# Centred-only transposes at the start, and attention pieces in front of score bursts, in a transformer layer on one core

## Chip, cores, metric

The kernel runs on one core of one Trainium2 chip. The metric is the device time of one execution in microseconds; medians of several executions are quoted. Spans in the profile are 1.5 to 2.0 us shorter than the timed execution. The record marks a run as slow when it is over 1.5% above the fastest of its kernel.

## The reference

One pre-norm layer in bf16 with 2048 tokens and width 1024: attention with 32 heads of 32 and a causal window of 256, then an MLP of width 3584 with SiLU, both with a residual.

```python
def _layernorm(x, axis=-1, eps=1e-5):
    m = jnp.mean(x, axis=axis, keepdims=True)
    v = jnp.var(x, axis=axis, keepdims=True)
    return (x - m) / jnp.sqrt(v + eps)
...
x = A_x
h = x + _A_ref(_layernorm(x, axis=-1), A_wqkv, A_wo)     # q, k, v; windowed softmax; wo
h2 = h + _B_ref(_layernorm(h, axis=-1), B_w1, B_w2)      # silu(h @ w1) @ w2
```

## The kernel before

Tokens go in four blocks of 512, each of four row tiles of 128. TensorE (PE) computes V (a `v_group` per row tile and half of the columns), then Q and K (`qk_group`), of block b+1 as dense 128x512 matmuls, and the attention of block b is sprinkled between them: *bursts* of scores (tiles of 32 rows) and *pieces* of attention output (33 columns each). Block 0 has nothing to hide behind: its row tiles must be normalized and transposed first. Tiles 0 to 2 are transposed on PE, tile 3 by DMA.

```python
    load_x(0, 0)
    load_wqkv(2 * D)                 # first half of the V columns, 1 MB
    load_x(0, 1, nc.scalar)          # issued from ScalarE's queue
    load_x(0, 2)
    load_wqkv(2 * D + 512)
    load_x(0, 3)
    load_wqkv(0)
...  # 11 warm-up matmuls
    ln_stats(x_ring[0], st, 0)
    ln_root(st, rs, 0)
...
    v_group(0, 1, 0, act, turn_1_rest)
    ln_first(x_ring[2], st, rs, 2, 1)
    ln_stats(x_ring[3], st, 3)
    ln_root(st, rs, 3)
    ln_first(x_ring[3], st, rs, 3, 1)
    ln_transpose(x_ring[3], lnT_b[0], 3)      # by DMA
    for c0 in (D, 512, D + 512):
        load_wqkv(c0)
...
    for j in range(4):
        load_x(1, j)                          # block 1
...
    class Stream:
        def between(self, kt):                # called before each dense matmul
            if self.seen * self.n >= self.done * 192:
                self.bursts[self.done]()
                self.done += 1
            if self.seen * self.n * 2 >= (self.given * 2 + 1) * 192:   # halfway between bursts
                if pending:
                    pending.pop(0)()                                   # a piece
...
```

While Q and K of block 0 run, VectorE takes the statistics of block 1 in the same queue as the evacuations (copies of finished results out of PSUM) of the odd Q/K groups. Two PSUM banks serve these groups in turn.

The softmax here doesn't subtract the row's maximum and nothing guards it: scores larger than these inputs give would overflow.

Of the kernel before, what the change touches and what calls it, by code (L numbers as in the profile page):

```python
# [9 lines left out]
F32 = mybir.dt.float32  # L10
I32 = mybir.dt.int32
ACT = mybir.ActivationFunctionType
ALU = mybir.AluOpType

P = 128
# [29 lines left out]
def kernel(  # L45
# [49 lines left out]
    def view(region, off, *dims):  # L95
        n = 1
        for d in dims:
            n *= d
        ap = region[:, off:off + n]
        if len(dims) == 2:  # L100
            return ap.rearrange("p (a b) -> p a b", b=dims[1])
        if len(dims) == 3:
            return ap.rearrange("p (a b c) -> p a b c", b=dims[1], c=dims[2])
        return ap
# [29 lines left out]
    def load_x(b, j, queue=nc.sync):  # L134
        queue.dma_start(out=x_ring[(b % 2) * 4 + j], in_=x2d[(b * 4 + j) * P:(b * 4 + j + 1) * P, :])  # L135

    def load_wqkv(c0):
        dst = wqk[:, :, c0:c0 + 512] if c0 < 2 * D else wv[:, :, c0 - 2 * D:c0 - 2 * D + 512]
        nc.sync.dma_start(out=dst, in_=wqkv_v[:, :, c0:c0 + 512])

    eps = const.tile([P, 1], F32, name="eps")
    nc.vector.memset(eps[:], LN_EPS)
# [1 line left out]
    nc.scalar.activation(out=dummy[:], in_=eps[:], func=ACT.Sqrt)  # L144

    load_x(0, 0)
    load_wqkv(2 * D)
    load_x(0, 1, nc.scalar)
    load_x(0, 2)
    load_wqkv(2 * D + 512)  # L150
    load_x(0, 3)
    load_wqkv(0)

    ident = const.tile([P, P], BF16, name="ident")
    make_identity(nc, ident[:])
    warm = view(r_e, 0, 2, 512)
    nc.vector.memset(warm, 0.0)
    nc.gpsimd.memset(v[:, :, :, DH:VW], 1.0)


    for i in range(11):
        nc.tensor.matmul(o_ps[i % 2][:].rearrange("p a b -> p (a b)"), lhsT=warm[:, 0, 0:P], rhs=warm[:, 0, :], start=True, stop=True)


    def ln_half(xt, stats, c):
# [27 lines left out]
    def ln_norm(xt, st, rs, j):  # L193
        nc.vector.tensor_scalar(out=xt, in0=xt, scalar1=st[:, j, 0:1], scalar2=rs[:, j:j + 1],
                                op0=ALU.subtract, op1=ALU.mult)
# [4 lines left out]
    def ln_root(st, rs, j):  # L200
        nc.scalar.activation(out=rs[:, j:j + 1], in_=st[:, j, 1:2], func=ACT.Sqrt, bias=eps[:], scale=1.0)

    def ln_first(xt, st, rs, j, parts, on_act=0):

        if on_act:
            shift = small.tile([P, 2], F32, name="ln_shift", tag="ln_shift")
            nc.scalar.activation(out=shift[:, 0:1], in_=st[:, j, 0:1], func=ACT.Identity, scale=-1.0)
        nc.vector.reciprocal(out=rs[:, j:j + 1], in_=rs[:, j:j + 1])
        if on_act:
            nc.scalar.activation(out=shift[:, 1:2], in_=shift[:, 0:1], func=ACT.Identity, scale=rs[:, j:j + 1])  # L210
        n = 1024 // parts
        for h in range(parts):
            part = xt[:, h * n:(h + 1) * n]
            if h < parts - on_act:
                ln_norm(part, st, rs, j)
            else:
                nc.scalar.activation(out=part, in_=part, func=ACT.Identity, bias=shift[:, 1:2], scale=rs[:, j:j + 1])

    def turn_first(j, h):

        for i in range(2):
            kt = h * 2 + i
            nc.tensor.transpose(out=tp_ps[h][:, i * P:(i + 1) * P], in_=x_ring[j][:, kt * P:(kt + 1) * P], identity=ident[:])  # L223
        nc.scalar.copy(out=lnT_b[0][:, h * 2:(h + 1) * 2, j * P:(j + 1) * P],
                       in_=tp_ps[h][:, 0:256].rearrange("p (k q) -> p k q", q=P))

# [193 lines left out]
    class Stream:  # L420
# [1 line left out]


        def __init__(self, b):
            self.bursts, self.pieces, self.done, self.given, self.seen = [], [], 0, 0, 0
            self.behind = 2 if b else 1
            pending.extend(coming)
            coming.clear()
            for g in range(0, G, 2):
                if b:  # L430
                    self.bursts += [lambda g=g: scores_c(b, g)]
                    self.bursts += [lambda g=g, k=k, o=o: scores_xy(b, g + k, o) for k in range(2) for o in range(2)]
                    self.pieces += [lambda g=g, s=s: attn_piece(b, g, *s) for s in SPLIT]
                else:
                    self.bursts += [lambda g=g, k=k, o=o: scores_0(g + k, o) for k in range(2) for o in range(2)]
                    self.pieces += [lambda g=g, k=k: attn_piece(b, g, k, k + 8) for k in range(0, 32, 8)]
            self.n = len(self.bursts)

        def between(self, kt):
            if self.seen * self.n >= self.done * 192:  # L440
                self.bursts[self.done]()
                self.done += 1
            if self.seen * self.n * 2 >= (self.given * 2 + 1) * 192:
                if pending:
                    pending.pop(0)()
                coming.append(self.pieces[self.given])
                if len(coming) > self.behind:
                    pending.append(coming.pop(0))
                self.given += 1
            self.seen += 1  # L450

    dve, act = nc.vector.tensor_copy, nc.scalar.copy


    st, rs = ln_tiles("a")
    half = small.tile([P, 2, 6], F32, name="ln_st", tag="ln_st")
    ln_stats(x_ring[0], st, 0)
    ln_root(st, rs, 0)
    ln_half(x_ring[1], half, 0)
    ln_first(x_ring[0], st, rs, 0, 4, 1)  # L460
    ln_stats(x_ring[1], st, 1, half)
    for h in range(4):
        turn_first(0, h)
        if h == 2:
            ln_root(st, rs, 1)
    ln_first(x_ring[1], st, rs, 1, 4)
    ln_stats(x_ring[2], st, 2)

    held = []

    def turn_1(kt):
        if kt == 7:
            turn_first(1, 0)

    def turn_1_rest(kt):
        if kt == 2:
            turn_first(1, 3)
            act(**held.pop())
            ln_root(st, rs, 2)

    v_group(0, 0, 0, lambda **args: held.append(args), turn_1)
    turn_first(1, 1)
    turn_first(1, 2)
    v_group(0, 1, 0, act, turn_1_rest)
    ln_first(x_ring[2], st, rs, 2, 1)
    ln_stats(x_ring[3], st, 3)
    ln_root(st, rs, 3)
    ln_first(x_ring[3], st, rs, 3, 1)
    ln_transpose(x_ring[3], lnT_b[0], 3)
    for c0 in (D, 512, D + 512):  # L490
        load_wqkv(c0)
    v_group(0, 0, 1, act)
    for h in range(4):
        turn_first(2, h)
    v_group(0, 1, 1, act)
    v_group(0, 2, 0, act)
    v_group(0, 2, 1, act)
    nc.scalar.activation(out=dummy[:], in_=eps[:], func=ACT.Exp)
    v_group(0, 3, 0, act)
    v_group(0, 3, 1, act)  # L500

    ps_tp.__exit__(None, None, None)
    ps_sc = tc.tile_pool(name="ps_sc", bufs=1, space=bass.MemoryType.PSUM, reuse_waits="tile")
# [138 lines left out]
    for b in range(NB):  # L642
        extra = []
        if b == 0:
            extra = [(f, 1) for f in pending]
            pending = []
        for ft in range(FT):
            acc = h1_group(b, ft)
            run_late()
            if extra:  # L650
                extra.pop(0)[0]()
            if b == 0 and ft == 3:
                for i in (1, 2, 3, 4):
                    load_w2(i)
            silu(b, acc, ft)
            if b == 0 and 6 <= ft < 14:
                j, c = divmod(ft - 6, 2)
                wo_group(NB - 1, j, c)
        load_h(b, 0)
        if b == 0:  # L660
            load_w2(6)
        steps = ln2_steps(b + 1) if b + 1 < NB else []
        def mm2(acc, j, c0, c1, first, last):
            for ft in range(first, last):
                nc.tensor.matmul(acc[:, 0:c1 - c0], lhsT=gT[:, ft, j * P:(j + 1) * P], rhs=w2[ft // 4][:, ft % 4, c0:c1],  # L665
                                 start=(ft == 0), stop=(ft == FT - 1))

        for j in range(4):
            if j < 3:
                load_h(b, j + 1)  # L670
            cols = [(0, 512), (512, 1024)]
            if b == NB - 1 and j == 3:
                cols = [(0, 512), (512, 768), (768, 896), (896, 1024)]
            accs = [next_acc() for _ in cols]
            early = FT - 4 if b == 0 and j == 0 else 0
            for acc, (c0, c1) in zip(accs, cols):
                mm2(acc, j, c0, c1, 0, early)
            for acc, (c0, c1) in zip(accs, cols):
                mm2(acc, j, c0, c1, early, FT)
                nc.vector.scalar_tensor_tensor(out=t_out[j % 2][:, c0:c1], in0=acc[:, 0:c1 - c0], scalar=0.5,  # L680
                                               in1=t_in[j % 2][:, c0:c1], op0=ALU.mult, op1=ALU.add)
                nc.sync.dma_start(out=out2d[(b * 4 + j) * P:(b * 4 + j + 1) * P, c0:c1], in_=t_out[j % 2][:, c0:c1])
                for _ in range(3):
                    if steps:
                        steps.pop(0)()
        while steps:
            steps.pop(0)()
# [30 lines left out]
```

## Time and profile before

| | before |
|---|---|
| time, median of 3 runs | 692.93 us |
| PE busy | 98% of 691.4 us |
| first V matmul starts | 7.92 us |
| first Q/K matmul starts | 22.82 us |
| first score burst | 50.54 us |

In the lines of a timeline the columns are start, duration (both us), engine and source line, operation, output and input tiles, shapes and count; in square brackets stands the idle time before the first of them and what ended it. The durations of matmuls are modelled: what counts are starts. Consecutive lines of one kind are merged into one.

The last 40 V matmuls, tiles 2 and 3 among them, run without a wait up to the first of Q/K:

```profile
14.19 8.80 PE L245 MATMUL acc<-r_w 128*128 128x512 bf16 x40
```

### The profile page before, as it was taken

What the parts mean: (1) busy time and instruction counts of PE and PEld (TensorE: products, weight loads), DVE (VectorE), ACT (ScalarE), POOL (GpSimd) and SP (SyncE); (2) the same over time, 40 slices, a digit from 0 to 9 for tenths busy, and PEclk for the clock granted to TensorE, in tenths of its full rate; (3) what the DMA queues carried; (4) which work ended last, traced back from release to release, by engine and by line L of the source; (5) the groups of instructions that cost most, each with busy time, mean ns of one, the idle gap of its engine ahead of it and who ended that gap; (6) DMA issues with size and microseconds to landing.
All of it is one profiled execution on the core that took longest, in us unless ns stands there. A gap on an engine that the chain in (4) does not pass through costs nothing.

```text
span 691.4 us, 14107 instructions
## 1 busy us (share of the span) xinstructions
PE 677.0 (98%) x5895; PEld 331.6 (48%) x6011; DVE 290.5 (42%) x609; ACT 241.8 (35%) x463; POOL 160.4 (23%) x295
## 2 busy tenths in 40 slices
PE   8999999999999999999999999999999999999998
PEld 3444455555555555544444444444444444444445
DVE  5267646744444439534315133343133251333111
ACT  5326666766666666421310033300133100233000
POOL 1007666656666666500000000000000000000000
PEclk9999999999999999999999999999999999999999
DMA  8732242136241889971023410022300024100110
GB/s 251 251 55 78 39 80 61 26 63 183 73 131 17 241 235 281 213 277 50 12 80 111 93 39 0 1 91 69 85 0 1 17 95 95 39 1 1 30 39 24
DMA packets 76463, 60.95 MB, mean 88 GB/s; under 512 B 50288, under 2 KB 60528, under 8 KB 76400
## 3 DMA queue, kind: packets, MB, share of 16 engines
q1 hardware_dynamic: 76256, 59.78, 32.0%
q8 instruction: 47, 0.77, 0.5%
q10 hardware_dynamic: 144, 0.26, 0.1%
q14 instruction: 16, 0.13, 0.1%
HBM read 39.85 MB, written 8.39 MB: 70 GB/s over the span
## 4 chain that ended last, share of the span: by engine, by line
PE 97%; issue 1%; DMA 1%; SPq 0%; DVE 0%
PE hacc L628 19%; PE hacc L665 17%; PE acc L255 16%; PE acc L665 10%; PE acc L628 9%; PE acc L245 8%; PE acc L276 7%; PE o_ps L388 5%; PE sc L308 3%; PE hacc L276 1%; DMA r_w<-in_A_wqkv_dram 1%; PE sc L360 1%; PE sc L334 1%; PE tp L223 0%; SPq L135 0%
## 5 line engine op out<-in xcount | busy, mean ns | idle before, releaser
L378 POOL TENSOR_SCALAR_AFFINE_SELECT r_e<-r_e 128x512 bf16<-128x512 bf16 (+1 forms) x288 | 157.4, 561 | 126.6 <-ACT r_e L368 62.7
L665 PEld LDWEIGHTS <-r_a 128*128 128x128 bf16 x952 | 90.9, 98 | 103.0
L628 PEld LDWEIGHTS <-r_w 128*128 128x128 bf16 x896 | 87.4, 98 | 105.0 <-issue 0.2
L665 PE MATMUL hacc<-r_a 128*128 128x512 bf16 (+2 forms) x607 | 121.8, 359 | 0.5
L628 PE MATMUL hacc<-r_e,r_w 128*128 128x512 bf16 x444 | 99.7, 379 | 0.5
L320 ACT ACTIVATE r_e<-sc 128x768 bf16<-128x768 f32 x96 | 78.2, 814 | 48.3 <-PE sc L308 47.6
L637 ACT ACTIVATE r_n<-hacc 128x512 f32<-128x512 f32 x30 | 17.9, 597 | 178.9 <-PE hacc L628 175.5
L665 PE MATMUL acc<-r_a 128*128 128x512 bf16 x329 | 73.5, 379 | 0.4
L255 PEld LDWEIGHTS <-r_w 128*128 128x128 bf16 x512 | 44.2, 97 | 46.1 <-issue 1.0
L255 PE MATMUL acc<-r_t,r_w 128*128 128x512 bf16 x233 | 60.3, 379 | 2.4 <-issue 1.7
L257 DVE CAST r_a<-acc 128x512 bf16<-128x512 f32 x56 | 38.6, 690 | 56.6 <-PE acc L255 43.8
L255 PE MATMUL acc<-r_w 128*128 128x512 bf16 x240 | 58.0, 379 | 1.5 <-issue 0.9
L388 PEld LDWEIGHTS <-r_e 128*128 128x128 bf16 x1440 | 47.4, 96 | 17.9
L276 PE MATMUL acc<-r_o,r_a 128*128 128x512 bf16 x188 | 49.5, 379 | 1.9 <-issue 1.3
L628 PE MATMUL acc<-r_e,r_w 128*128 128x512 bf16 x213 | 48.9, 379 | 0.3
L388 PE MATMUL o_ps<-r_a,r_e 128*128 128x33 bf16 x1440 | 48.1, 178 | 0.1
L321 ACT ACTIVATE r_e<-sc 128x256 bf16<-128x256 f32 x96 | 37.6, 392 | 0.0
L680 DVE SCALAR_TENSOR_TENSOR r_t<-hacc,r_t 128x512 bf16<-128x512 f32 (+2 forms) x22 | 14.0, 635 | 55.2 <-PE hacc L665 53.8
L680 DVE SCALAR_TENSOR_TENSOR r_t<-acc,r_t 128x512 bf16<-128x512 f32 x12 | 8.3, 692 | 64.2 <-PE acc L665 58.8
L638 DVE SCALAR_TENSOR_TENSOR r_a<-r_n,hacc 128x512 bf16<-128x512 f32 x30 | 20.6, 688 | 33.0 <-ACT r_n L637 33.0
L628 PE MATMUL hacc<-r_a,r_w 128*128 128x512 bf16 x139 | 32.6, 379 | 0.3
L276 PEld LDWEIGHTS <-r_a 128*128 128x128 bf16 x256 | 21.8, 97 | 22.3
(79 smaller groups left out, 532.5 us busy)
## 6 DMA issues: line engine op xcount, KB each, us to landing
r_w<-in_B_w_dram SPq DMA_DIRECT2D x8, 896.0 KB, 5.2
r_a<-in_B_w_dram SPq DMA_DIRECT2D x7, 1024.0 KB, 7.5
r_w<-in_A_wqkv_dram SPq DMA_DIRECT2D x6, 1024.0 KB, 9.3
h_dram<-r_t SPq DMA_DIRECT2D x16, 256.0 KB, 2.5
r_t<-h_dram SPq DMA_DIRECT2D x16, 256.0 KB, 2.9
out_dram<-r_t SPq DMA_DIRECT2D x31, 128.0 KB, 1.7
r_o<-in_A_x_dram SPq DMA_DIRECT2D x15, 256.0 KB, 4.2
r_e<-h_dram SPq DMA_DIRECT2D x3, 1024.0 KB, 5.7
```

The source lines that it names most:

```text
L245: nc.tensor.matmul(acc, lhsT=lnT_b[b % 2][:, kt, j * P:(j + 1) * P], rhs=wv[:, kt, c * 512:(c + 1) * 512], start=(kt == 0), stop=(kt == KT ...
L255: nc.tensor.matmul(acc, lhsT=wqk[:, kt, col0:col0 + P], rhs=lnT_b[b % 2][:, kt, :], start=(kt == 0), stop=(kt == KT - 1))
L257: copy(out=(qT, kT)[which][b][:, g, :], in_=acc)
L276: nc.tensor.matmul(acc, lhsT=qT[b][:, g, j * P:(j + 1) * P], rhs=wo[:, g, c * 512:(c + 1) * 512], start=(g == 0), stop=(g == G - 1))
L308: nc.tensor.matmul(sc[hh // 2][half * 64:half * 64 + 64, hh % 2, col:col + qb - qa], lhsT=kT[t // 4][r0:r0 + DH, g, k0:k0 + 64], rhs=qT[b] ...
L320: nc.scalar.activation(out=tri[:, :, :, 64:256], in_=both, func=ACT.Exp, scale=scale)
L321: nc.scalar.activation(out=e[:, 1024:1280].rearrange("p (h q) -> p h q", q=P), in_=bank[:, :, 192:320], func=ACT.Exp, scale=scale)
L378: nc.gpsimd.affine_select(out=dst, in_=src, pattern=[[0, n] for n in dst.shape[1:-1]] + [[sgn, P]], compare_op=ALU.is_ge if upper else ALU ...
L388: nc.tensor.matmul(o_ps[pair][:, qt * 2 + hh, 0:VW], lhsT=chunk_of(i, bank, piece, pair, hh), rhs=v[:, b * 4 + kt, g * 4 + pair * 2 + hh, ...
L628: nc.tensor.matmul(acc, lhsT=w1[:, kt, ft * P:(ft + 1) * P], rhs=ln2T[b][:, kt, :], start=(kt == 0), stop=(kt == KT - 1))
L665: nc.tensor.matmul(acc[:, 0:c1 - c0], lhsT=gT[:, ft, j * P:(j + 1) * P], rhs=w2[ft // 4][:, ft % 4, c0:c1], start=(ft == 0), stop=(ft == F ...
L680: nc.vector.scalar_tensor_tensor(out=t_out[j % 2][:, c0:c1], in0=acc[:, 0:c1 - c0], scalar=0.5, in1=t_in[j % 2][:, c0:c1], op0=ALU.mult, o ...
```

## The change

Two parts. **Start:** row tiles 0 and 1 are only centred (the mean comes sooner than the variance), transposed, and V is multiplied by 1/std when its PSUM banks are evacuated; the V groups get four banks. Q and K need normalized rows, so tiles 0 and 1 are normalized later and transposed again, by DMA. In the code `hold` puts off a group's evacuation, `scaled` makes it up with the factor 1/std, and `place` puts transposes between the matmuls of a group. The loads are reordered and split. **Pieces:** each stands directly in front of a burst instead of halfway between two.

```diff
     load_x(0, 0)
-    load_wqkv(2 * D)
-    load_x(0, 1, nc.scalar)
+    load_x(0, 1)
+    load_wqkv(2 * D, 4)          # four loads of 256 KB
     load_x(0, 2)
-    load_wqkv(2 * D + 512)
+    load_wqkv(2 * D + 512, 2)
...
-    for i in range(11):
+    for i in range(9):           # warm-up
...
+    mean_first(); center(0); center(1)
+    v_group(0, 0, 0, hold, place({1: (0, 2), 3: (0, 3), 5: (1, 0), 6: (1, 1), 7: (1, 2)}))
...
+    v_group(0, 1, 0, hold)
+    v_group(0, 0, 1, hold)
+    scaled(0)                    # evacuate V, times 1/std
+    ln_recip(rs, 1)
+    scaled(1)
+    scaled(0)
+    ln_stats(x_ring[3], st, 3)
+    v_group(0, 1, 1, hold)
     for h in range(4):
-        turn_first(2, h)
+        turn_first(2, h, x_ring[2])
+        if h == 1:
+            ln_root(st, rs, 3)
+    scaled(1)
+    ln_norm(x_ring[0], st, rs, 0)
+    ln_recip(rs, 3)
+    ln_norm(x_ring[3], st, rs, 3)
+    ln_norm(x_ring[1], st, rs, 1)
+    for j in (3, 0, 1):
+        ln_transpose(x_ring[j], lnT_b[0], j)
     for c0 in (D, 512, D + 512):
         load_wqkv(c0)
...
         def between(self, kt):
             if self.seen * self.n >= self.done * 192:
-                self.bursts[self.done]()
-                self.done += 1
-            if self.seen * self.n * 2 >= (self.given * 2 + 1) * 192:
                 if pending:
                     pending.pop(0)()
-                coming.append(self.pieces[self.given])
+                self.bursts[self.done]()
+                coming.append(self.pieces[self.done])
...
-            if b == 0 and 6 <= ft < 14:       # last output groups inside the MLP
+            if b == 0 and 7 <= ft < 15:
```

More of the change, by code (lines that the diff above doesn't have):

```diff
@@ L135, in load_x, with load_wqkv @@
         queue.dma_start(out=x_ring[(b % 2) * 4 + j], in_=x2d[(b * 4 + j) * P:(b * 4 + j + 1) * P, :])
-    def load_wqkv(c0):
+    def load_wqkv(c0, parts=1):
         dst = wqk[:, :, c0:c0 + 512] if c0 < 2 * D else wv[:, :, c0 - 2 * D:c0 - 2 * D + 512]
-        nc.sync.dma_start(out=dst, in_=wqkv_v[:, :, c0:c0 + 512])
+        n = KT // parts
+        for k in range(0, KT, n):
+            nc.sync.dma_start(out=dst[:, k:k + n, :], in_=wqkv_v[:, k:k + n, c0:c0 + 512])
+    warm = view(r_e, 0, P)
+    nc.vector.memset(warm, 0.0)
     eps = const.tile([P, 1], F32, name="eps")
@@ L155 @@
     make_identity(nc, ident[:])
-    warm = view(r_e, 0, 2, 512)
-    nc.vector.memset(warm, 0.0)
     nc.gpsimd.memset(v[:, :, :, DH:VW], 1.0)
-    for i in range(11):
-        nc.tensor.matmul(o_ps[i % 2][:].rearrange("p a b -> p (a b)"), lhsT=warm[:, 0, 0:P], rhs=warm[:, 0, :], start=True, stop=True)
+    wide = bass.AP(tensor=warm.tensor, offset=warm.offset, ap=[warm.ap[0], [0, 4], warm.ap[1]])
+    for i in range(9):
+        nc.tensor.matmul(o_ps[i % 2][:].rearrange("p (a c) b -> p a (c b)", c=2), lhsT=warm, rhs=wide, start=True, stop=True)
     def ln_half(xt, stats, c):
@@ L201, in ln_root, with ln_recip, turn_first @@
         nc.scalar.activation(out=rs[:, j:j + 1], in_=st[:, j, 1:2], func=ACT.Sqrt, bias=eps[:], scale=1.0)
-    def ln_first(xt, st, rs, j, parts, on_act=0):
-        if on_act:
-            shift = small.tile([P, 2], F32, name="ln_shift", tag="ln_shift")
-            nc.scalar.activation(out=shift[:, 0:1], in_=st[:, j, 0:1], func=ACT.Identity, scale=-1.0)
+    def ln_recip(rs, j):
         nc.vector.reciprocal(out=rs[:, j:j + 1], in_=rs[:, j:j + 1])
-        if on_act:
-            nc.scalar.activation(out=shift[:, 1:2], in_=shift[:, 0:1], func=ACT.Identity, scale=rs[:, j:j + 1])
-        n = 1024 // parts
-        for h in range(parts):
-            part = xt[:, h * n:(h + 1) * n]
-            if h < parts - on_act:
-                ln_norm(part, st, rs, j)
-            else:
-                nc.scalar.activation(out=part, in_=part, func=ACT.Identity, bias=shift[:, 1:2], scale=rs[:, j:j + 1])
-    def turn_first(j, h):
+    def turn_first(j, h, src):
         for i in range(2):
             kt = h * 2 + i
-            nc.tensor.transpose(out=tp_ps[h][:, i * P:(i + 1) * P], in_=x_ring[j][:, kt * P:(kt + 1) * P], identity=ident[:])
+            nc.tensor.transpose(out=tp_ps[h][:, i * P:(i + 1) * P], in_=src[:, kt * P:(kt + 1) * P], identity=ident[:])
         nc.scalar.copy(out=lnT_b[0][:, h * 2:(h + 1) * 2, j * P:(j + 1) * P],
@@ L424, in __init__ @@
         def __init__(self, b):
-            self.bursts, self.pieces, self.done, self.given, self.seen = [], [], 0, 0, 0
-            self.behind = 2 if b else 1
+            self.bursts, self.pieces, self.done, self.seen = [], [], 0, 0
+            self.behind = 3 if b else 2
             pending.extend(coming)
@@ L440, in between @@
             if self.seen * self.n >= self.done * 192:
-                self.bursts[self.done]()
-                self.done += 1
-            if self.seen * self.n * 2 >= (self.given * 2 + 1) * 192:
                 if pending:
                     pending.pop(0)()
-                coming.append(self.pieces[self.given])
+                self.bursts[self.done]()
+                coming.append(self.pieces[self.done])
                 if len(coming) > self.behind:
                     pending.append(coming.pop(0))
-                self.given += 1
+                self.done += 1
             self.seen += 1
@@ L455 @@
     st, rs = ln_tiles("a")
-    half = small.tile([P, 2, 6], F32, name="ln_st", tag="ln_st")
-    ln_stats(x_ring[0], st, 0)
-    ln_root(st, rs, 0)
-    ln_half(x_ring[1], half, 0)
-    ln_first(x_ring[0], st, rs, 0, 4, 1)
-    ln_stats(x_ring[1], st, 1, half)
-    for h in range(4):
-        turn_first(0, h)
-        if h == 2:
-            ln_root(st, rs, 1)
-    ln_first(x_ring[1], st, rs, 1, 4)
-    ln_stats(x_ring[2], st, 2)
-    held = []
-    def turn_1(kt):
-        if kt == 7:
-            turn_first(1, 0)
@@ L475, in turn_1_rest @@
-    def turn_1_rest(kt):
-        if kt == 2:
-            turn_first(1, 3)
-            act(**held.pop())
-            ln_root(st, rs, 2)
-    v_group(0, 0, 0, lambda **args: held.append(args), turn_1)
-    turn_first(1, 1)
-    turn_first(1, 2)
-    v_group(0, 1, 0, act, turn_1_rest)
-    ln_first(x_ring[2], st, rs, 2, 1)
-    ln_stats(x_ring[3], st, 3)
-    ln_root(st, rs, 3)
-    ln_first(x_ring[3], st, rs, 3, 1)
-    ln_transpose(x_ring[3], lnT_b[0], 3)
+    x_mid = [view(r_e, 1024 + 1024 * j, 1024) for j in range(2)]
@@ new lines, with mean_first @@
+    scrap = view(r_e, 3072, 1024)
+    mean = small.tile([P, 3], F32, name="mean")
+    half = small.tile([P, 2, 6], F32, name="ln_half")
+    def mean_first():
+        nc.scalar.activation(out=scrap[:, 0:512], in_=x_ring[0][:, 512:1024], func=ACT.Identity, scale=-1.0 / D, accum_out=mean[:, 0:1])
+        ln_half(x_ring[0], half, 0)
+        nc.vector.tensor_scalar(out=mean[:, 1:2], in0=half[:, 0, 1:2], scalar1=half[:, 0, 4:5], scalar2=-0.25, op0=ALU.add, op1=ALU.mult)
+        nc.scalar.activation(out=scrap, in_=x_ring[1], func=ACT.Identity, scale=-1.0 / D, accum_out=mean[:, 2:3])
@@ new lines, in center, with hold, scaled @@
+    def center(j):
+        for h in range(4):
+            out, in0 = (x[j][:, h * 256:(h + 1) * 256] for x in (x_mid, x_ring))
+            if j == 0:
+                nc.vector.tensor_scalar(out=out, in0=in0, scalar1=mean[:, 0:1], scalar2=mean[:, 1:2], op0=ALU.add, op1=ALU.add)
+            else:
+                nc.vector.tensor_scalar(out=out, in0=in0, scalar1=mean[:, 2:3], scalar2=None, op0=ALU.add)
+    held = []
+    def hold(**args):
+        held.append(args)
+    def scaled(j):
+        args = held.pop(0)
+        nc.scalar.activation(func=ACT.Identity, scale=rs[:, j:j + 1], **args)
@@ new lines, in place @@
+    def place(at):
+        return lambda kt: turn_first(*at[kt], x_mid[at[kt][0]]) if kt in at else None
+    acc_banks += [o[:].rearrange("p a b -> p (a b)") for o in o_ps]
+    mean_first()
+    center(0)
+    center(1)
+    turn_first(0, 0, x_mid[0])
+    turn_first(0, 1, x_mid[0])
+    v_group(0, 0, 0, hold, place({1: (0, 2), 3: (0, 3), 5: (1, 0), 6: (1, 1), 7: (1, 2)}))
+    turn_first(1, 3, x_mid[1])
+    ln_stats(x_ring[2], st, 2)
+    ln_root(st, rs, 2)
+    ln_stats(x_ring[0], st, 0, half)
@@ new lines @@
+    ln_root(st, rs, 0)
+    ln_recip(rs, 2)
+    ln_norm(x_ring[2], st, rs, 2)
+    ln_recip(rs, 0)
+    ln_stats(x_ring[1], st, 1)
+    ln_root(st, rs, 1)
+    v_group(0, 1, 0, hold)
[6 more added lines that the diff above has]
+    v_group(0, 1, 1, hold)
+    for h in range(4):
+        turn_first(2, h, x_ring[2])
[3 more added lines that the diff above has]
+    ln_norm(x_ring[0], st, rs, 0)
@@ L490 @@
+    ln_recip(rs, 3)
[3 more added lines that the diff above has]
+        ln_transpose(x_ring[j], lnT_b[0], j)
     for c0 in (D, 512, D + 512):
         load_wqkv(c0)
-    v_group(0, 0, 1, act)
-    for h in range(4):
-        turn_first(2, h)
-    v_group(0, 1, 1, act)
     v_group(0, 2, 0, act)
@@ L500 @@
     v_group(0, 3, 1, act)
+    del acc_banks[2:]
     ps_tp.__exit__(None, None, None)
@@ L651 @@
                 extra.pop(0)[0]()
-            if b == 0 and ft == 3:
+            if b == 0 and ft == 4:
                 for i in (1, 2, 3, 4):
@@ L655 @@
             silu(b, acc, ft)
-            if b == 0 and 6 <= ft < 14:
-                j, c = divmod(ft - 6, 2)
+            if b == 0 and 7 <= ft < 15:
+                j, c = divmod(ft - 7, 2)
                 wo_group(NB - 1, j, c)
```

## The prediction

> **What bounds the kernel now.** I read the page first: the engines' shares, the slices, and the chain that ended last.
>
> ```profile
> PE 677.0 (98%) x5895; PEld 331.6 (48%) x6011; DVE 290.5 (42%) x609; ACT 241.8 (35%) x463; POOL 160.4 (23%) x295
> ...
> PE   8999999999999999999999999999999999999998
> ...
> PE 97%; issue 1%; DMA 1%; SPq 0%; DVE 0%
> ```
>
> TensorE (PE) is busy in every slice and carries 97% of the chain, so time can only come from what it executes, from its switches, or from its two weak ends. The change removes two warm-up matmuls and no other PE work. It touches two stretches: the first 23 us, and the attention stages at 50 to 300 us.
>
> Next, the timeline of the first 45 us (start, duration, engine, line, operation, tiles, count; in brackets the wait before it).
>
> ```profile
> 4.25 1.29 DVE L166 BATCH_NORM_STATS2 ln_st<-r_o 128x6 f32<-128x512 bf16 x2 [2.76 <-DMA r_o<-in_A_x_dram]
> ...
> 6.84 0.93 PE L223 MATMUL tp<-ident,r_o 128*128 128x128 bf16 x8 [0.41 <-DVE r_o L194]
> ...
> 7.92 1.67 PE L245 MATMUL acc<-r_w 128*128 128x512 bf16 x7
> ...
> 9.73 1.28 DVE L166 BATCH_NORM_STATS2 ln_st<-r_o 128x6 f32<-128x512 bf16 x2
> ...
> 14.75 0.55 DVE L194 TENSOR_SCALAR r_o<-r_o,st_a,rs_a 128x1024 bf16<-128x1024 bf16 x1
> ...
> 15.32 1.34 SPq L198 DMA_TRANSPOSE r_w<-r_o  x1
> ...
> 22.82 22.39 PE L255 MATMUL acc<-r_w 128*128 128x512 bf16 x100
> ...
> 30.54 1.27 DVE L166 BATCH_NORM_STATS2 ln_st<-r_o 128x6 f32<-128x512 bf16 x2
> ```
>
> The reader is to see three things. The first V matmul is at 7.92, just after the first megabyte of wqkv has landed (7.87 in the trace's landing events), so the start is bound by transfers. Row tile 3 is normalized at 15.30, transposed by DMA from 15.32 and lands at 18.53, before V of tile 3 needs it at 19.37: slack 0.8 us. The Q/K groups begin at 22.82; from there PE steps at 216 ns without a gap. At 30.54 VectorE starts the statistics of block 1, whose first tile landed at 30.45: almost no slack.
>
> Then PE alone, in narrow timelines of an attention stage:
>
> ```profile
> 177.53 0.59 PE L245 MATMUL acc<-r_w,r_t 128*128 128x512 bf16 x2
> 178.06 0.33 PE L308 MATMUL sc<-r_a 32*64 32x320 bf16 x4
> ...
> 179.08 0.59 PE L245 MATMUL acc<-r_w,r_t 128*128 128x512 bf16 x2
> 179.51 0.18 PE L388 MATMUL o_ps<-r_a,r_e 128*128 128x33 bf16 x1
> ...
> 179.91 0.35 PE L388 MATMUL o_ps<-r_a,r_e 128*128 128x33 bf16 x8
> 180.12 0.38 PE L245 MATMUL acc<-r_w,r_t 128*128 128x512 bf16 x1
> ```
>
> The dense matmuls start 0.216 apart, so the second of the pair at 177.53 starts at 177.75 and the scores follow 0.31 later. From all start times of the trace, medians: dense to dense 216 ns, dense to score burst 309 (311 for the C bursts; 76 of them), dense to attention piece 216, piece to dense 25, score burst to dense 120 where the burst ends on 64 columns, 147 where on 128. Only the score bursts cost a switch; the pieces enter and leave free. No burst waits for its PSUM banks: the 309 doesn't vary by more than 1 ns.
>
> **What the Trainium skill says.** "TensorEngine Tiling (Array Packing)", Key Properties: changing the tiling mode drains the TensorE. The trace agrees: scores use 32-row tiles and cost about 93 ns extra on entering (309-216) and on leaving (147-53, 120-27); pieces use the whole array and cost none. "TensorE: Matmul & The Clock Gate", Back-to-back issue gap: N/2.4 + 2.5 ns when warm, with an issue floor near 25 ns for small N. It agrees: 216 at 512 columns, 25 at 33. The same page, Part 1, says that the clock is released by a sustained busy window of about 3.4 us; here the recorded full clock begins at about 6.75 us, after eleven warm-up matmuls spaced 427 ns. "DMA: Bandwidth & Descriptors", Where 436 GB/s comes from: about 358 GB/s of HBM per core; the landings show some 355 in this start.
>
> **Part 1, pieces in front of bursts.** Per burst, before: dense to piece 216, piece to dense 25, dense to burst 309, sum 550. After: dense to piece 216, piece to burst X, dense to dense 216. The switch fits N/2.4 + 94 ns for N = 64, 128 and 512 (120, 147, 309 in turn), so a piece, whose last matmul has 33 columns, should give X = 14+94 = 108, sum 540. That is 10 ns each. Counting pops in the code, 72 of 76 bursts have a piece in front (the first three of block 0 and one of block 1 have none): **-0.7 us**. If the drain were wholly hidden, X = 25 and the gain 93x72 = 6.7 us; I give that 1 in 10. Expected: 0.9x(-0.7) + 0.1x(-6.7) = **-1.3 us**. Delays of pieces behind their bursts grow from 2.5 and 3.5 to 3 and 4 intervals, so selections and exps get more slack; ring buffers still come free before the burst that overwrites them. The fourth left-over piece moves into the MLP without cost, as would the last output groups, one step later.
>
> **Part 2, start.** PE no longer waits for 1/std: with x at about 4.0, a half-row sum on each of ScalarE and VectorE (0.65 to 0.8), the mean at 4.9 and a 0.29 us centring of a quarter, transposes start near 5.3 instead of 6.84, and V near 6.5 instead of 7.92 (ScalarE's 1024-element sum for tile 1 comes ahead of the first copy; an estimate of 1.2 us, from 0.81 for 768 elements). V of tiles 0, 1 then runs to about 14.2, with the landings of the second megabyte (about 10.1 and 11.6) met nearly without wait.
>
> But VectorE has more to do before tile 3: x2 lands at about 8.55 as now, because the same bytes go ahead of it. From there: stats of x2 1.28, aggregate 0.2, half stats of x0 0.64, aggregate 0.2, reciprocal 0.15, normalize x2 0.55, reciprocal 0.15, stats of x1 1.28, aggregate 0.2, root and reciprocal 0.5, stats of x3 1.28, aggregate 0.2, normalize x0 0.55: with the small gaps 15.85. The root of tile 3 on ScalarE stands behind three scaled evacuations (0.6 each from 13.6) and two copies (0.3 each), so it ends at 16.2; reciprocal and normalize give 17.0 (now 15.3). The DMA transpose of tile 3 then lands at 17.0+3.2 = 20.2, while V of tile 2 is over at about 19.2. V of tile 3 takes sixteen times 0.216 from 20.25, and Q/K begin at about 23.7: **+0.9 us**. The transposes of tiles 0 and 1 (issues of 1.34 each) land at 21.6 and 23.0, just in time.
>
> A second consequence: the three wqkv loads and the loads of block 1 stand behind three transposes instead of one on the same queue, 21.2 instead of 16.7, so block 1's first tile lands near 34.9 instead of 30.45. VectorE takes its statistics ahead of the evacuation of Q/K group 5: 34.9 + 1.28 + 0.2 + 0.69 = 37.1, but group 7, which reuses that bank, could start at 23.7 + 7x1.73 = 35.8. A stall of 1.3 us. The late landing before was partly one DMA engine lagging 2 us behind the others (landing counts of a load spread over 2 us), so I weigh it at 6 in 10: **+0.8 us**.
>
> Sum: 692.9 - 1.3 + 0.9 + 0.8 = **693.3 us**.
>
> **Rivals.** *The start really gains.* If the root of tile 3 and the DMA transpose come 1 us earlier than I chain them, V of tile 3 doesn't wait, Q/K start at 22.4, and with block 1 in time the whole is 692.9-0.4-0.7 = 691.8. For it: PE's work is ready earlier. Against: every duration in VectorE's chain is measured. *VectorE and the SP queue become the bound of the start*, in full: +0.9+1.35-0.7 gives 694.5; evacuations with a pointer scale may take 0.1 longer each (the one-column activation with a pointer took 0.29, without 0.19), +0.3 more. *The drain disappears*: with X = 25 about 688 to 689, if the start costs little. *The clock is released a window later*, because nine warm-up matmuls end near 4.9 and PE is then half idle until 7.5: early V matmuls at 427 ns; mostly hidden behind transfers and ScalarE, perhaps +0.5. *Queue starvation*: 24 pairs of a piece and 24 of a burst in a row; the stage now averages some 115 instructions in 2.9 us without starving, so I expect none.
>
> **Range and chances.** The terms range from -6.7 to 0 and from -0.4 to +2.8, with extremes unlikely together: 690.5 to 696.0 for 8 in 10. Two per cent is 13.9 us; no path above reaches it, so within 2% gets 0.98.
>
> **What would show it.** Piece to burst near 108 ns (rival: 25), dense to burst 309 only in the four bursts without a piece. First transpose near 5.3, first V matmul near 6.5, full clock before 7. The normalization of tile 3 ending near 17.0, its transpose landing near 20.2, PE idle about 1 us before V of tile 3, the first Q/K matmul near 23.7. A PE gap near 36 with VectorE waiting for x. If instead Q/K start before 22.8, my VectorE chain is wrong; if the attention stages shrink by over 2 us, my drain formula is.

## The result

The changed kernel takes 695.18 us (694.60 to 695.45, four runs) against 692.94 (692.86 to 693.03, four runs). A ratio in this document is the record's own, of the fast runs of two kernels in the same rounds; it is not quite the ratio of the medians (1.0032 here). It is 1.0029, with a 95% interval of 1.0015 to 1.0043. The change makes the kernel slower by 2.0 us (by this ratio) to 2.2 us (by the medians). That is the same by the 2% measure, inside the range of the prediction, and 1.9 us above its point.

The page of the changed kernel shows the same amount of PE work and a chain in which PE has lost three points to other engines (shares and busy times first, then the chain):

```profile
PE 677.0 (98%) x5894; PEld 342.5 (49%) x6009; DVE 292.2 (42%) x613; ACT 243.4 (35%) x464; POOL 160.8 (23%) x295
...
PE 94%; DMA 2%; issue 1%; SPq 1%; DVE 1%; ACT 0%
```

Its timeline of the first 45 us, the lines on the path:

```profile
6.74 0.38 PE L236 MATMUL acc<-r_w 128*128 128x512 bf16 x1 [1.22 <-DMA r_w<-in_A_wqkv_dram]
...
9.57 1.29 DVE L170 BATCH_NORM_STATS2 ln_st<-r_o 128x6 f32<-128x512 bf16 x2 [3.10 <-DMA r_o<-in_A_x_dram]
...
16.84 0.31 ACT L205 ACTIVATE rs_a<-st_a,eps 128x1 f32<-128x1 f32 x1
...
17.37 1.00 DVE L198 TENSOR_SCALAR r_o<-r_o,st_a,rs_a 128x1024 bf16<-128x1024 bf16 x2
...
17.95 4.14 SPq L202 DMA_TRANSPOSE r_w<-r_o  x3
...
21.26 1.90 PE L236 MATMUL o_ps<-r_w 128*128 128x512 bf16 x8 [0.90 <-DMA r_w<-r_o]
...
24.72 12.25 PE L246 MATMUL acc<-r_w 128*128 128x512 bf16 x54
...
35.72 1.29 DVE L170 BATCH_NORM_STATS2 ln_st<-r_o 128x6 f32<-128x512 bf16 x2 [3.20 <-DMA r_o<-in_A_x_dram]
...
37.17 0.64 DVE L248 CAST r_a<-acc 128x512 bf16<-128x512 f32 x1
...
37.86 7.50 PE L246 MATMUL acc<-r_w 128*128 128x512 bf16 x34 [0.89 <-DVE r_a L248]
```

V begins at 6.74, 1.18 us sooner than before, and yet Q/K begin at 24.72, 1.90 us later. In between, tile 3's root (16.84), normalization (17.37) and DMA transpose (from 17.95, landing at 21.21) follow one another, and V of tile 3 waits for the last of these at 21.26. The second loss is at 37.86: VectorE sat 3.20 us waiting for block 1's x (landing at 35.70), the evacuation behind those statistics came at 37.17, and PE waited for its bank. The last matmul before the gap starts at 36.59, so 37.86-36.59-0.22 = 1.05 us are lost.

The pieces, in a narrow timeline of the same kernel:

```profile
285.83 0.18 PE L379 MATMUL o_ps<-r_a,r_e 128*128 128x33 bf16 x1
285.94 0.43 PE L299 MATMUL sc<-r_a 32*64 32x320 bf16 x24
```

From a piece's last matmul to a burst there are 0.11 us. By all start times: about 107 ns in 60 cases and about 110 in the 12 C bursts (those of the function `scores_c`); dense to burst is left 4 times, at 309.

| PE starts, us | before | changed | difference |
|---|---|---|---|
| first V | 7.92 | 6.74 | -1.18 |
| first Q/K | 22.82 | 24.72 | +1.90 |
| first score burst | 50.54 | 53.49 | +2.95 |
| second MLP matmul, first weights | 349.64 | 352.15 | +2.51 |
| span | 691.39 | 693.74 | +2.35 |

So the loss arises in two steps before 50 us, 1.90 and 1.05, and the attention stretch gives 0.44 back. This profile is of the slowest of the four runs. In the profile of the repeat, `a_same`, the steps are smaller: Q/K begin at 24.20 (+1.38), the gap is 0.89, the first burst comes at 52.80 (+2.26), and the span is 1.72 longer than before.

### The profile page after: what moved, and what is told of

The parts are those of the page before. It is cut to its first block, busy times and chain, and to the rows that moved or that the text cites. A ratio compares the mean times of both kernels' runs of the same rounds, so it can differ in the third digit from the quotient of the medians.

```text
span 693.7 us, 14121 instructions
## 1 busy us (share of the span) xinstructions
PE 677.0 (98%) x5894; PEld 342.5 (49%) x6009; DVE 292.2 (42%) x613; ACT 243.4 (35%) x464; POOL 160.8 (23%) x295
## 4 chain that ended last, share of the span: by engine, by line
PE 94%; DMA 2%; issue 1%; SPq 1%; DVE 1%; ACT 0%
PE hacc L648 19%; PE hacc L685 17%; PE acc L246 14%; PE acc L685 10%; PE acc L648 9%; PE acc L236 7%; PE acc L267 7%; PE o_ps L379 5%; PE sc L299 3%; DMA r_o<-in_A_x_dram 2%; PE hacc L267 1%; PE sc L351 1%; DMA r_w<-in_A_wqkv_dram 1%; PE sc L325 1%; SPq L202 1%
## 5 line engine op out<-in xcount | busy, mean ns | idle before, releaser
L685 PEld LDWEIGHTS <-r_a 128*128 128x128 bf16 x952 | 90.9, 98 | 103.0
L648 PEld LDWEIGHTS <-r_w 128*128 128x128 bf16 x896 | 87.3, 98 | 105.0 <-issue 0.4
L246 PEld LDWEIGHTS <-r_w 128*128 128x128 bf16 x512 | 47.1, 98 | 56.1 <-issue 2.2
L246 PE MATMUL acc<-r_t,r_w 128*128 128x512 bf16 x233 | 56.5, 380 | 2.4 <-issue 1.7
L246 PE MATMUL acc<-r_w 128*128 128x512 bf16 x240 | 56.1, 379 | 2.4 <-issue 1.0
L267 PE MATMUL acc<-r_o,r_a 128*128 128x512 bf16 x188 | 46.2, 380 | 1.9 <-issue 1.3
L267 PEld LDWEIGHTS <-r_a 128*128 128x128 bf16 x256 | 23.4, 98 | 26.9
```

The lines of the kernel that those rows point to most:

```text
L246: nc.tensor.matmul(acc, lhsT=wqk[:, kt, col0:col0 + P], rhs=lnT_b[b % 2][:, kt, :], start=(kt == 0), stop=(kt == KT - 1))
L267: nc.tensor.matmul(acc, lhsT=qT[b][:, g, j * P:(j + 1) * P], rhs=wo[:, g, c * 512:(c + 1) * 512], start=(g == 0), stop=(g == G - 1))
L648: nc.tensor.matmul(acc, lhsT=w1[:, kt, ft * P:(ft + 1) * P], rhs=ln2T[b][:, kt, :], start=(kt == 0), stop=(kt == KT - 1))
L685: nc.tensor.matmul(acc[:, 0:c1 - c0], lhsT=gT[:, ft, j * P:(j + 1) * P], rhs=w2[ft // 4][:, ft % 4, c0:c1], start=(ft == 0), stop=(ft == F ...
```

## The experiments

My theory: the start of the change costs, through two waits that stand in a row; the pieces save a little. Rivals: the pieces cost; the array clock, which in the changed kernel's first profile drops to half between 7.15 and 10.56 us, costs; the gap at 37 is hidden again later. Every kernel below gave correct results. They were timed in three calls, each on another chip, with the kernel before in the same rounds; its medians there were 693.10, 693.10 and 693.12 us.

### The parts apart: `b_pieces`, `b_pieces2`, `a_oldpieces`, `a_same`

`b_pieces` is the kernel before with the second part of the diff alone; `a_oldpieces` is the changed kernel with that part undone; `b_pieces2` and `a_same` repeat `b_pieces` and the changed kernel, unaltered.

> The kernel before with only the second part of the change: each attention piece directly in front of a score burst (and the last output groups of the MLP's first block one step later). Theory (the switch costs N/2.4 + 94 ns after the last matmul, so a 33-column piece in front saves about 10 ns in each of 72 bursts): piece to burst 107 to 110 ns in the trace, and the whole 0.4 to 0.8 us shorter, about 692.3. Rival 1 (the pieces' move is what costs the 2.2 us of the full change, for instance by later softmax results): 694 or more. Rival 2 (the start stretch alone makes the full change slower and the pieces save several us that the start hides): 690 or less.

> The changed kernel with the old places of the pieces: the start of the change alone. Theory (the start costs: Q/K begin 1.9 us later, and about 1.05 us more are lost where block 1's statistics wait for their loads): about 0.5 us longer than the changed kernel, 695.4 to 696.2, with the gap near 37 us unchanged. Rival (the pieces cause the loss): back near 693.

> The kernel before with the pieces moved alone, again, for a comparison with the repaired kernel on the same chip and rounds: 692.3 to 692.7, ratio 0.9992 to before.

> The changed kernel again, unaltered, for the same chip and rounds as the other three of this call. Expected from its first runs: 694.6 to 695.5, ratio 1.0029 to before; V of tile 3 waiting about 0.9 us for the DMA transpose and the gap of about 1 us near 37. Whether the array clock drops for one period early on, as in its first profile (full from 3.7, half from 7.15 to 10.56), is open; the theory says that it changes the whole by under 0.5 us.

| run (5 runs each) | median us | range | ratio to before | 95% |
|---|---|---|---|---|
| b_pieces | 692.45 | 692.42 to 692.95 | 0.9992 | 0.9980 to 1.0005 |
| b_pieces2 | 692.98 | 692.30 to 693.17 | 0.9995 | 0.9983 to 1.0007 |
| a_oldpieces | 695.06 | 694.63 to 696.93 | 1.0033 | 1.0019 to 1.0047 |
| a_same | 694.85 | 694.81 to 695.59 | 1.0029 | 1.0016 to 1.0041 |

The loss belongs to the start: without the pieces' move it is still there (1.0033), and the move alone costs nothing. `a_oldpieces` came out below the 695.4 that I expected; the timed runs don't show it longer than the changed kernel. The gain of the pieces' move, 0.3 to 0.6 us by the ratios, has the expected sign but an interval that holds 1 (and the median of `b_pieces2` is above what I expected), so the timing alone doesn't prove it; what proves the mechanism is the trace, where piece to burst is 107 and 110 ns in `b_pieces` too. From the first burst to the first weights of the second MLP matmul `b_pieces` takes 298.52 us, the kernel before 299.10: 0.57 less (the formula's 72 times 11 ns would give 0.8).

Over all profiles: the three kernels with the old places need 299.10 us for this stretch, six of the eleven with the new places 298.52 to 298.59, three more 298.66 to 298.77. The last two, `b_pieces2` (299.13) and `a_parts1` (299.26), lost the gain again in one place, 0.6 and 0.75 us ahead of the first MLP matmul. In `a_parts1` the profile puts this wait down to the DMA transpose of the MLP's input (`r_a<-r_a`), which lands 0.25 us before that matmul. In `b_pieces2` it names nobody, but the same transpose lands 0.20 before it (285.62 and 285.82), where in `b_pieces` it had landed 0.46 before and PE did not wait. So PE, now earlier, can catch up with this transpose; no run tests it.

### The first wait: `a_root3`

```diff
     ln_stats(x_ring[3], st, 3)
+    ln_root(st, rs, 3)
     v_group(0, 1, 1, hold)
     for h in range(4):
         turn_first(2, h, x_ring[2])
-        if h == 1:
-            ln_root(st, rs, 3)
```

> The changed kernel with one instruction moved: the root of tile 3 on ScalarE right after tile 3's statistics are emitted, ahead of the copies of tile 2's transposes. Theory (V of tile 3 waits for a chain VectorE, ScalarE root, VectorE, DMA transpose): the root runs near 16.1 instead of 16.84, tile 3 is normalized near 17.1 instead of 17.9, its DMA transpose lands near 20.4 instead of 21.2, and Q/K begin about 0.8 us earlier; the whole 0.6 to 0.9 us shorter. Rival (V of tile 3 is late because PE itself lost time at half clock before 10.6 us): no change of the whole, a longer wait before V of tile 2 or 3 somewhere else.

Measured: 694.15 us (693.65 to 694.84), ratio 1.0016 (1.0003 to 1.0028). In its timeline the root, the transposes' issue, V of tile 3 and Q/K:

```profile
15.81 0.29 ACT L205 ACTIVATE rs_a<-st_a,eps 128x1 f32<-128x1 f32 x1
...
16.91 4.12 SPq L202 DMA_TRANSPOSE r_w<-r_o  x3
...
20.25 1.90 PE L236 MATMUL o_ps<-r_w 128*128 128x512 bf16 x8 [0.21 <-DMA r_w<-r_o]
...
23.72 12.25 PE L246 MATMUL acc<-r_w 128*128 128x512 bf16 x56
```

The order of one 0.3 us instruction on an engine that is 35% busy moves the start of Q/K from 24.72 to 23.72. Counted from x2's landing, which differs between profiles, it is 14.35 us here, 15.17 in the changed kernel's first profile and 14.91 in its repeat, so 0.6 to 0.8 us are gained. The time follows: 0.7 us below the repeat of the changed kernel. It was run on another chip. V of tile 3 waits for this chain.

### The second wait: `a_xearly`

```diff
-    for c0 in (D, 512, D + 512):
-        load_wqkv(c0)
+    load_wqkv(D)
+    for j in range(4):
+        load_x(1, j)
+    load_wqkv(512)
+    load_wqkv(D + 512)
```

> The changed kernel with the four loads of block 1's x issued directly after the wqkv load of column D, ahead of those of columns 512 and D+512 (3 MB of wqkv no longer stand before them). Theory (the second loss is group 7 of Q/K waiting for an evacuation that stands behind statistics that wait for x): block 1's first tile lands near 29 instead of 35.7, PE's gap of 1.05 us near 37 is gone, Q/K begin as before at about 24.7, and the whole is 0.9 to 1.2 us shorter. Rival (the gap near 37 is given back later, in slack): no change of the whole.

Measured: 693.62 us (693.33 to 694.87), ratio 1.0011 (0.9998 to 1.0023). Block 1's first tile lands at 27.76, VectorE no longer waits for it, and PE runs from the first Q/K matmul without a break:

```profile
24.07 16.14 PE L246 MATMUL acc<-r_w 128*128 128x512 bf16 x74
...
31.78 1.28 DVE L170 BATCH_NORM_STATS2 ln_st<-r_o 128x6 f32<-128x512 bf16 x2
```

That is 1.2 us less than the repeat of the changed kernel. It was run on another chip. `a_oldpieces` is 1.4 us longer; part of that is the pieces. The gap at 37 was on the path and is not given back later.

The late landing of block 1's x has a second part, which my prediction had noticed in the kernel before. A load reports its landing in 16 counts in the trace, and what waits for it goes on after the last. In all 14 profiles one 16 KB packet of the kind "instruction" appears in DMA queue 8 in this stretch (at 28.71 us in the changed kernel, 22.87 before) and takes 1.05 to 1.14 us. The first of the late wqkv loads lands before it, its counts 0.22 to 0.59 us apart; loads that land after its end have their last count 1.58 to 2.02 us behind their first, whichever queue x1 was loaded from. For block 1's first tile in the changed kernel that is 1.72 us, more than the gap. That the packet makes the lag is inferred from this order alone; no run tests it.

### Where x2's late landing comes from: `a_parts1`, `a_actq`, `b_x1sync`

My chain began with x2 landing at 8.55, as before. It landed at 9.55. The last of the 16 landing counts of that load came 1.72 us after the first; before, 0.67. No instruction packet lies between 0.2 and 20 us in any profile, so this lag needs another cause. I suspected the split loads first.

```diff
 a_parts1:
-    load_wqkv(2 * D, 4)
+    load_wqkv(2 * D)
-    load_wqkv(2 * D + 512, 2)
+    load_wqkv(2 * D + 512)
 a_actq:
-    load_x(0, 1)
+    load_x(0, 1, nc.scalar)
 b_x1sync (in the kernel before):
-    load_wqkv(2 * D)
-    load_x(0, 1, nc.scalar)
+    load_x(0, 1)
+    load_wqkv(2 * D)
```

> The changed kernel with the first two wqkv columns loaded whole again (1 MB each, not four and two parts). In all five profiles with parts x2's load lands at 9.2 to 9.55 us, its first and its last of 16 counts 1.2 to 1.7 us apart; in both without, at 8.4 to 8.55, 0.7 apart, though the same bytes stand before it. Theory (the parts make the late engine): x2 lands near 8.5, VectorE's chain, the transpose of tile 3 and the start of Q/K all come about 0.7 earlier (near 23.7), although the first V matmul comes later (near 7.8 instead of 5.9 to 6.7); the whole about 0.7 us shorter than the changed kernel. Rival (x1 on the same queue makes it late, or chance): x2 still lands after 9.1, and the whole is the same or longer, since V now waits for all of the first column.

> The changed kernel with the load of x1 on ScalarE's queue again, as before; the parts stay. Theory (parts make the late engine): x2 still lands after 9.1, no change of the whole. Rival (x1 on the same queue makes it late): x2 lands near 8.5 and the whole is about 0.7 us shorter.

> The kernel before with only x1's load moved from ScalarE's queue to the SP queue, in the changed kernel's order (x0, x1, first wqkv column). Theory (a start whose loads all stand in one queue lets one of the 16 counts of each load come 1.2 to 2.7 us late): the first column lands after 9 instead of 7.87, the first V matmul follows it, x2 lands after 9.1, and the whole is 0.7 to 1.7 us longer. Rival (the lateness belongs to the changed kernel's other differences): 692.9 to 693.4.

| run | median us | range | ratio to before | x2 lands | first to last count |
|---|---|---|---|---|---|
| a_parts1 | 698.68 | 696.58 to 699.58 | 1.0078 | 10.29 | 2.75 |
| a_actq | 693.46 | 693.34 to 694.27 | 1.0009 | 8.28 | 0.50 |
| b_x1sync | 695.97 | 695.48 to 698.43 | 1.0049 | 9.35 | 1.76 |

My theory fell, and plainly: whole loads made it worse by 3.8 us against `a_same`. The rival holds: x1 on ScalarE's queue brings x2 back to 8.28 and saves 1.4 us, and the same move alone, made in the kernel before, costs 2.9 us, more than the 0.7 to 1.7 that I had put, though the first column landed at 8.65 and not after 9. Part of the 2.9 may be the clock: the record has it below full speed in all six of its runs (0.995 to 0.998; 1.000 in all runs of `a_actq` and `a_same`). In `a_actq` x2's load was issued 0.47 us earlier than in `a_same`, but its first count did not come earlier (7.78 and 7.69); only the last ones did. The three kernels of the kernel-before kind with x1 on ScalarE's queue, `a_actq` and `a_best` below land x2 at 8.28 to 8.55; of the nine profiles with x1 in the SP queue, eight land it at 9.22 to 10.29 and one at 8.46. Why a second queue for one 256 KB load keeps some of the 16 counts of the next loads from lagging, no run shows.

What the split loads are good for is seen here as well. The first V matmul of each (timelines of `a_parts1`, `a_actq`, `b_x1sync`, in this order):

```profile
9.63 0.59 PE L236 MATMUL acc<-r_w 128*128 128x512 bf16 x1 [3.81 <-DMA r_w<-in_A_wqkv_dram]
```

```profile
6.19 0.39 PE L236 MATMUL acc<-r_w 128*128 128x512 bf16 x1 [0.22 <-ACT r_w L215]
```

```profile
8.69 3.05 PE L245 MATMUL acc<-r_w 128*128 128x512 bf16 x7 [1.66 <-DMA r_w<-in_A_wqkv_dram]
```

With whole loads and a lagging last part, V waits 3.81 us; with parts and the second queue it waits 0.22 us, and that for ScalarE's copy of its transposed rows, as the change intends.

### The clock: `a_warm`

```diff
-    for i in range(9):
+    for i in range(13):
```

> The changed kernel with 13 warm-up matmuls instead of 9, so that TensorE stays busy until the first transposes and the loads. Theory (the early drop of the array clock, seen in one of two profiles of the changed kernel, hides behind VectorE's chain): no clock drop in the profile, and the whole within 0.5 us of the changed kernel, 694.5 to 695.3. Rival (the drop is a main part of the loss): 694 or less.

Measured: 694.35 us (693.64 to 695.03), ratio 1.0018 (1.0006 to 1.0030): between the two theories' numbers, below my 694.5 and above the rival's 694, so by itself inconclusive; its profile also happened to be the one in which x2 landed early (8.46). V began at 7.20 in it, a microsecond later than in `a_same` (6.25), but Q/K, counted from x2's landing, only 0.2 us later (15.11 and 14.91). What speaks against the clock as a main cause is that it dropped in one of two profiles of the changed kernel, and in none of `a_oldpieces`, `a_root3` or `a_xearly`. The timed runs say the same: of the nine runs of the changed kernel the record has a clock below full speed in one alone, the profiled one (0.997, 695.45 us); the other eight took 694.60 to 695.59. (A run without clock records counts as full speed there.) `a_oldpieces` has the full loss (1.0033), and its profile Q/K at 24.25 and the gap near 37. Where the clock does drop, PE runs at half rate: V matmuls start 0.427 us apart in the changed kernel's first profile (8.06 and 8.48), 0.216 apart in `a_same` (9.29 and 9.50), whose trace holds no clock record, so that its 1.00 below is only a default. Stretches of three profiles (the changed kernel's first, `a_same`, `a_parts1`; the columns are the stretch and its length, busy time and count of PE, PEld, DVE, ACT and POOL, then the granted clock, the share of the DMA engines and GB/s):

```profile
7.20:10.50 3.30, 3.30 (x16) 1.64 (x14) 0.93 (x2) 1.49 (x4) 0.00 (x0) 0.50 1.02 347
```

```profile
7.20:10.50 3.30, 2.85 (x21) 1.53 (x19) 1.19 (x2) 1.75 (x5) 0.00 (x0) 1.00 1.01 348
```

```profile
7.20:10.50 3.30, 0.87 (x4) 0.47 (x4) 0.18 (x1) 0.03 (x1) 0.00 (x0) 0.50 1.03 348
```

Between the changed kernel's first profile (dropped) and `a_same` (not), Q/K begin at 24.72 and 24.20; 0.26 of that is x2's landing (9.55 and 9.29). So in the changed kernel a drop is worth a few tenths. In `a_parts1` and `b_x1sync` V itself is late and then runs at half clock. Two runs of `a_parts1` for which no drop is recorded took 696.58 and 698.78, the three others 698.50 to 699.58, so most of its loss is there without a drop; for `b_x1sync`, where all six runs have one, the two were not separated.

### The repairs together: `a_both`, `a_best`

`a_both` has the edits of `a_root3` and `a_xearly`; `a_best` adds that of `a_actq`.

> The changed kernel with both repairs: the root of tile 3 earlier, and block 1's x loaded ahead of two wqkv columns. Theory (two losses in a row, each on the path): the gains add, 0.9 and 1.4 us, so 692.9 to 693.3, Q/K near 23.6 and no gap near 36. Rival (they overlap: one hides the other): no better than the better of the two alone, 693.6.

> The changed kernel with all three repairs that helped alone: x1's load on ScalarE's queue, tile 3's root earlier, block 1's x loaded ahead of two wqkv columns. Theory (three waits on one path): x2 lands near 8.3, tile 3's transpose near 19.3, Q/K begin near 22.7 (before: 22.8), no gap near 35, and the whole is 692.1 to 692.6, the same as the kernel before with the pieces moved alone: the new start then gains nothing over the old. Rival (the early V work pays once the waits are gone): 691.8 or less. Other rival (the repairs overlap, as the two of the previous call did in their timed runs): 693 or more.

`a_both`: 693.57 us (693.10 to 694.12), ratio 1.0009 (0.9996 to 1.0022). It missed the expectation: no better than `a_xearly` alone. In its profile both repairs work (V of tile 3 waits 0.22 us, no gap near 36), but x2 landed at 9.60, the latest of all but `a_parts1`, and Q/K begin at 23.97. Counted from x2's landing, the first burst comes after 43.9 in the changed kernel (43.5 in its repeat), 42.9 in `a_root3`, 42.6 in `a_xearly` and 42.1 in `a_both`, so in the traces the gains nearly add; in the timed runs I can't show it.

`a_best`: 692.46 us (692.04 to 692.74), ratio 0.9989 (0.9977 to 1.0002). Its timeline:

```profile
8.52 1.29 DVE L170 BATCH_NORM_STATS2 ln_st<-r_o 128x6 f32<-128x512 bf16 x2 [1.70 <-DMA r_o<-in_A_x_dram]
...
16.04 4.13 SPq L202 DMA_TRANSPOSE r_w<-r_o  x3
...
19.39 1.90 PE L236 MATMUL o_ps<-r_w 128*128 128x512 bf16 x8 [0.22 <-DMA r_w<-r_o]
...
22.86 22.18 PE L246 MATMUL acc<-r_w 128*128 128x512 bf16 x100
```

With all three waits gone, Q/K begin at 22.86, against 22.82 before, though V began at 6.18 instead of 7.92. So the three waits account for the whole loss, and at Q/K the new start has gained nothing over the old. What is left, 0.8 us of gain by the ratio, is not distinguishable from what the pieces give alone (0.3 to 0.6). No kernel here beats the kernel before by more than the noise; the best medians, 692.45 and 692.46, are `b_pieces` and `a_best`.

## Why the prediction was right or wrong

- **What bounds it, and where the change acts.** Right: the differences arise before 50 us and in the attention stretch, but for 0.16 us by which the rest is shorter and which nothing here explains.
- **Pieces.** Right in mechanism and nearly in size: X was predicted at 108 ns and measured at 107 (110 for the C bursts), and 72 bursts have a piece in front, 4 have none. The formula's 0.7 us came out as 0.44 in the first profile and 0.57 in `b_pieces`. The rival of a wholly hidden drain (X = 25) is refuted; weighting it at 1 in 10 put 0.6 us of false gain into the sum, and that is the first mis-sized term: -1.3 predicted, about -0.5 measured.
- **VectorE's chain to tile 3.** Right: from the start of x2's statistics to the issue of tile 3's transpose I chained 17.0-8.58 = 8.4 us, and the trace has 17.95-9.57 = 8.4. Root behind three scaled evacuations and two copies, transpose landing 3.2 us after its issue, V of tile 3 waiting about 1 us: all as put. `a_root3` shows that it is the path.
- **"x2 lands at about 8.55 as now, because the same bytes go ahead of it."** Wrong, and it is the step that failed: 9.55 in this profile, 9.29 in the repeat. The same bytes land later when x1 stands in the same queue as the others. It turned +0.9 us at Q/K into +1.9 (+1.4 in the repeat). `a_actq` and `b_x1sync` show it in both kernels.
- **Second consequence, block 1's loads.** Right in mechanism, and undersized by my weighting: +0.8 in the sum, 1.05 measured (0.89 in the repeat). x landed at 35.70 where I had 34.9; the transposes had been issued 0.95 later than I put, which is the same late start. `a_xearly` shows it.
- **Clock rival.** Its effect, early V matmuls at 427 ns, came in the first profile, but not by the way I described: the clock was not released a window later but early, at 3.73, and fell back at 7.15. It was not the cause of the loss in the changed kernel.
- **Queue starvation.** Did not occur: a piece and a burst in a row ran at their usual spacing.

In the first profile the sum that was measured is +1.9 (Q/K), +1.05 (gap), -0.44 (attention): 2.5 by the second MLP matmul and 2.35 in the span. The rival "VectorE and the SP queue become the bound of the start", 694.5, was the true course; my point of 693.3 averaged it away. All three errors point the same way: 0.8 us of gain too much for the pieces, 1.0 too little loss for x2, 0.25 too little for the gap.

## What to carry to other kernels

Starting the bottleneck engine sooner gained nothing here, because the last input of that stage still came at its old time (in `a_best` V began 1.7 us sooner and Q/K at the same time): follow each chain that must end before the *next* stage, and see what the new work puts in front of it. Look at what stands behind the work that is moved to a DMA queue: here three transposes, which started 2.6 us later and took 2.8 us longer to issue than the one before, moved the loads behind them from 16.71 to 22.13, and so a stage that begins 18 us after them. Put a small instruction that feeds a long chain (here a one-column root) ahead of the copies on its engine, not behind them; it was worth 0.6 to 0.8 us at Q/K.

## What the Trainium skill lacked or had wrong

- "Trainium Kernel Development and Optimization", Key Constraints, says that issuing DMAs from several engines only saves issue time. Here the queue of one 256 KB load decided when later loads landed: x2 at 8.28 instead of 9.29 us, with the counts of one load 0.50 instead of 1.60 us apart (`a_actq` against `a_same`), and 1.4 us of the whole. The earlier issue does not explain it: the first count came no earlier (7.78 and 7.69).
- "TensorE: Matmul & The Clock Gate", Why this matters for your kernels, warns of PE-idle gaps over about 3 us. Here the clock dropped at 7.15 after only 2.4 us without ordinary matmuls (4.31 to 6.74), with four transposes in them; Part 4 of the page does say that transposes don't count as busy in the same way. In `a_actq` and `a_both`, whose clock was released at the same time (3.75 and 3.73), it stayed, with gaps of 1.87 and 1.78 us that held four transposes too.
- "TensorEngine Tiling (Array Packing)", Key Properties, says that a switch of mode drains the array, and gives no cost. The traces show the last matmul's columns at 2.4 a nanosecond plus 94 ns, for 33, 64, 128 and 512 columns (107, 120, 147, 309 ns).
